# Joining two words of a weight: the low word's top bits made on GpSimd, the join in one VectorE step

## The chip, the cores and the metric

The kernel runs on one core of a Trainium2 chip. The metric is the device time of one execution in microseconds (us); 753.64 us is the median of 3 runs of the kernel before (752.62 to 755.04). TensorE (PE) multiplies, with weight loads (PEld) beside it; VectorE (DVE), ScalarE (ACT) and GpSimd (POOL) do elementwise work; SyncE (SP) issues the DMAs. Every engine takes its own instructions in the order in which they were written and waits on semaphores of the others.

## The reference

Three layers follow one another. Inputs are float32; the weight matrices of both networks reach the chip as float64 (two 32-bit words a number).

```python
scores = scale * np.matmul(q, k.transpose(0, 1, 3, 2))     # 4 batches, 8 heads, 576 x 576, dim 64
attn = softmax(where(local mask or strided mask, scores, -1e9))
x = np.matmul(attn, v)                                      # 2304 x 512 after the heads are joined
h = np.maximum(np.maximum(x @ w1, x @ w2), x @ w3)          # 512 -> 768, three gates
x2 = h @ w_out                                              # 768 -> 512
h = x2 @ w_in                                               # 512 -> 2048
g = np.maximum(h, 0.0) + alpha * np.minimum(h, 0.0)
out = g @ moe2_w_out                                        # 2048 -> 512
```

## The kernel before, in words

**Stages.** The first stage, on PE up to about 320 us, is called the weave here. In it PE works through the attention of all four batches and the gate network of batches 0 to 2 (`gate_products`, L577, and `out1_products`, L599), while every weight of the program is converted once. Then `last_net` does batch 3 (L577, L750, L599), and from about 390 us on the second network runs (L1152, L983); it reads its converted weights back from DRAM. GpSimd works only in the masks at the start and, from 329 us on, in sums and splits of the input of the second network (L211, L828).

**Products.** A float32 number is held as two float32r parts, high and low, and a product is three matmuls (high-high, low-high, high-low).

**Converting a weight.** `from_double` adds the steps for a tile of 128 x 512 weights. `fetch` loads 512 KB into a tile of the `raw` ring (3 tiles). `rebase_words` (L448, ACT) rescales the upper word. `join_words` (L452 and L454, DVE) shifts that upper word left by 3 and then ORs in the lower word shifted right by 29: the tile `word` then holds the float32. There are 56 such tiles in all. Then `split_tasks` makes the high part (L253, ACT) and the low part (L256, DVE). The first 24 tiles stay in SBUF as gate and mix weights; of the others, sums of quarters are formed (L521, L560, DVE), and the parts go through a staging ring `wst` of 3 tiles back to DRAM (`wh`, `wo`, `wp`, `ws`).

**What sets the order.** The weave is written by a planner, `Weave.plan`. Each task has an engine with a cost in ns, a position that says how urgent it is, needs, and rings of buffers (8 PSUM banks, 3 raw tiles and so on). The planner walks through time, always takes the engine whose next task can begin first, and emits the tasks in that order; for some tasks it picks ACT or DVE, whichever would end first. The join had a cost of 1050 ns on DVE. `UNREAD` puts 3 and 9 matmuls whose result nobody reads (L359) ahead of two transposes of the first batch.

**Attention of one unit** (a batch, a pair of heads, a half): scores (L314, PE), mask and maximum (L322, DVE), exponential (L329, ACT), normalise (L351 on ACT or L353 on DVE), transposes (L364, PE), copies out of PSUM into `pt` (L253), values (L389, PE), and the split of the result `x` (L253 ACT, L256 DVE). The first gate product needs `x` of six units of batch 0 and one converted weight.

Of the kernel before, what the change touches and what calls it, by code (L numbers as in the profile page):

```python
# [10 lines left out]
F32 = mybir.dt.float32  # L11
F32R = mybir.dt.float32r
U32 = mybir.dt.uint32
AF = mybir.ActivationFunctionType
ALU = mybir.AluOpType

# [31 lines left out]
class Weave:  # L48
# [16 lines left out]
    def add(self, engines, emit, pos, needs=(), gives=(), makes=(), uses=(), mode=None, slack=0):  # L65
        t = len(self.tasks)
        if engines[0][0] != "PE" and any(key in self.banks for key in uses):
            pos -= self.URGENT
        self.banks.update(key for ring, key in makes if ring == "bank")
        self.tasks.append((engines, emit, pos, needs, makes, mode, slack))  # L70
        for ring, key in makes:
            if ring in self.order:
                self.order[ring].append(key)
        for e in gives:
            self.givers.setdefault(e, []).append(t)
        for key in [key for _, key in makes] + list(uses):
            self.users.setdefault(key, []).append(t)
# [19 lines left out]
    def plan(self, seed=None, near=120, change=100, slack=1.0, delay=350, shift=0.0):  # L97

        rng = random.Random(seed)
        sway = [rng.uniform(-shift, shift) if task[2] > -self.URGENT / 2 else 0.0 for task in self.tasks]  # L100
        delays = {"PE": 300, "ACT": delay, "DVE": delay, "SP": 2300}
        self.made = {ring: [] for ring in self.rings}
        free = dict.fromkeys(delays, 0)
        left = [sum(len(self.givers[e]) for e in task[3]) for task in self.tasks]
        at = [0] * len(self.tasks)
        ready = {t for t, n in enumerate(left) if not n}
        done, mode, order = {}, None, []
        while ready:
            options = {}
            for t in ready:  # L110
                engines, _, pos, _, makes, m, wait = self.tasks[t]
                when = self.place(makes, done)
                if when is None:
                    continue
                when = max(when, at[t] + slack * wait)
                best = None
                for e, cost in engines:
                    start = max(when, free[e])
                    if best is None or start + cost < best[0] + best[2]:
                        best = (start, e, cost)  # L120
                start, e, cost = best
                if m is not None:
                    start += change * (m != mode)
                options.setdefault(e, []).append(
                    (start, pos + sway[t] - (m is not None and m == mode), t, cost))
            pick = None
            for e, c in options.items():
                first = min(o[0] for o in c)
                o = min((o for o in c if o[0] <= first + near), key=lambda o: (o[1], o[0], o[2]))
                if pick is None or o[0] < pick[1][0]:  # L130
                    pick = (e, o)
            e, (start, _, t, cost) = pick
            makes, m = self.tasks[t][4:6]
            ready.remove(t)
            order.append((t, e))
            for ring, key in makes:
                self.made[ring].append(key)
            mode = mode if m is None else m
            free[e] = start + cost
            done[t] = start + cost + delays[e]  # L140
            for u in self.takers.get(t, ()):
                left[u] -= 1
                same = e == "PE" == self.tasks[u][0][0][0]
                at[u] = max(at[u], start + cost if same else done[t])
                if not left[u]:
                    ready.add(u)
        assert len(done) == len(self.tasks)
        return order
# [12 lines left out]
def attention_maxout_prelu_kernel(  # L161
# [13 lines left out]
    nc = tc.nc  # L175
# [74 lines left out]
    add, tl = weave.add, {}  # L250
# [13 lines left out]
    def load(kb):  # L264
        return (("SP", 3 * kb),)
# [30 lines left out]
    def attention_tasks(b, cc, hf, pos, step):  # L296
# [22 lines left out]
        for i, (_, _, _, m) in enumerate(tiles):  # L319
# [7 lines left out]
            def exponential(_, i=i):  # L327
                for j in range(2):
                    nc.scalar.activation(tl[ek][:nq, j, i, :nk], tl[ek][:nq, j, i, :nk], AF.Exp,  # L329
                                         bias=tl["nm", u][:nq, j, i:i + 1], scale=-1.0,  # L330
# [13 lines left out]
        for j in range(2):  # L344
            trk, ptk = ("tr", u, j), ("pt", u, j)

            def normalise(engine, j=j):
                e, rc = tl[ek][:nq, j, :n, :nk], tl["rc", u][:nq, j, :n]
                if engine == "ACT":
                    for i in range(n):  # L350
                        nc.scalar.activation(e[:, i], e[:, i], AF.Copy, scale=rc[:, i:i + 1])  # L351
                else:
# [68 lines left out]
    def from_double(key, src, pos, pace, after=()):  # L421

        rk, ak = ("raw", key), ("word", key)  # L430

        def fetch(_):
            raw = tl[rk] = raw_p.tile([P, DM, 2], U32, tag="raw", name="raw")
            nc.sync.dma_start(raw.rearrange("p n t -> p (n t)"), src.bitcast(U32))

        def rebase(_):
            tl[ak] = words_p.tile([P, DM], U32, tag="word", name="word")
            rebase_words(tl[rk], tl[ak])

        add(load(512), fetch, pos - 3 * pace, gives=[rk], makes=[("raw", rk)])  # L440
        add((("ACT", 570),), rebase, pos, needs=[rk, *after], gives=[("up", key)], makes=[("word", ak)],
            uses=[rk])
        add((("DVE", 1050),), lambda _: join_words(tl[rk], tl[ak]), pos, needs=[("up", key)],
            gives=[ak], uses=[rk, ak])
        return ak

    def rebase_words(raw, a):
        nc.scalar.activation(a.bitcast(F32), raw[:, :, 1].bitcast(F32), AF.Prelu, scale=2.0 ** -112,  # L448
                             alpha=-(2.0 ** 32))

    def join_words(raw, a):
        nc.vector.tensor_scalar(out=a, in0=a, scalar1=3, scalar2=None,  # L452
                                op0=ALU.logical_shift_left)
        nc.vector.scalar_tensor_tensor(out=a, in0=raw[:, :, 0], scalar=29, in1=a,  # L454
                                       op0=ALU.logical_shift_right, op1=ALU.bitwise_or)

    def split_tasks(key, ak, view, n, tile_of, pos, makes=(), given=None):

# [11 lines left out]
    def stay_tasks(key, src, pool, pos, pace):  # L470

        def tile_of():
            t = words[key] = pool.tile([P, 2, DM], F32R, tag="w", name="w")
            return t
        ak = from_double(key, src, pos, pace)
        split_tasks(key, ak, lambda a: a, DM, tile_of, pos)
# [22 lines left out]
    def pair_tasks(s, pos, pace):  # L499

        layer, q = divmod(s, NQ)
        ek, ok = (from_double(("in", layer, f), w2[f, layer], pos + pace * (f - 2 * q), pace,
                              [("sums", s - 2)] if s > 1 else ())
                  for f in (2 * q, 2 * q + 1))
# [4 lines left out]
        def sums(_):  # L509
            for k in sk:  # L510
                tl[k] = words_p.tile([P, DM], U32, tag="word", name="word")
            (e1, e2), (a1, a2), (c1, c2), (d, _) = (
# [28 lines left out]
    def factor_tasks(k, pos):  # L541
# [4 lines left out]
        for key, gk in zip(keys, (("gate", 2 * p, g), ("gate", 2 * p + 1, g))):  # L546
            def recover(_, key=key, gk=gk):
                tl[key] = words_p.tile([P, DM], U32, tag="word", name="word")
                w = words[gk].bitcast(F32)
                nc.vector.tensor_tensor(out=tl[key].bitcast(F32), in0=w[:, 0], in1=w[:, 1], op=ALU.add)  # L550
# [3 lines left out]
        def sums(_):  # L554
            tl[keys[2]] = words_p.tile([P, DM], U32, tag="word", name="word")
            (e1, e2), (a1, a2), (c1, c2) = ((t[:, :half], t[:, half:]) for t in
                                            (tl[key].bitcast(F32) for key in keys))
            for out_, x, y, op in ((c1, e1, a1, ALU.subtract), (a1, a1, a2, ALU.add),
                                   (c2, a1, e1, ALU.subtract), (a2, e2, c2, ALU.subtract)):
                nc.vector.tensor_tensor(out=out_, in0=x, in1=y, op=op)  # L560
# [360 lines left out]
    def temp():  # L921
        return tq.tile([P, HALF], F32, tag="t", name="t")
# [174 lines left out]
    def hidden(n, j, half, h):  # L1097

        f = 2 * (n % NQ) + j
        a = acts[j, half] = temp()  # L1100
        nc.scalar.activation(a, h, AF.Relu, scale=-1.0)  # L1101
        nc.scalar.activation(a, a, AF.Copy, scale=nalpha[:, f:f + 1])  # L1102

# [190 lines left out]
```

## Time and profile before

| | |
|---|---|
| median of 3 runs | 753.64 us (752.62 to 755.04) |
| the profiled execution's own time | 756.32 us |
| its span | 754.50 us, so 1.82 us lie around it |
| granted clock of PE over the span | 0.998 of full |
| PE busy | 737.3 us, 98% |
| VectorE busy | 630.6 us, 84% |
| ScalarE busy | 462.5 us, 61% |
| GpSimd busy | 53.3 us, 7% |
| first matmul | 4.82 us, first gate product 38.72 us |

The span is the time from the first to the last instruction that the profiler saw. Busy shares are means over stages with unlike limits, so the stretches have to be looked at one by one. A row of the timeline reads: start, length, engine, line, operation, output and inputs, shapes, count, and in brackets the idle time before it with what ended it. A row by line reads: count, then busy time in us and mean ns of one, then idle time before the group.

### The profile page before, as it was taken

How to read it: one execution, taken by the hardware profiler on the slowest of the kernel's cores; microseconds unless marked ns; L12 is line 12 of the kernel's file. 1: busy time of each engine (PE TensorE's matmuls, PEld its weight loads, DVE VectorE, ACT ScalarE, POOL GpSimd, SP SyncE). 2: the span in 40 equal slices, each digit the busy share in tenths (PEclk: the TensorE clock that was granted, in tenths of full speed). 3: DMA queues.
4: the chain of work that ended last, by engine and by line, in shares of the span. 5: the costliest groups of instructions: out<-in, count | busy, mean ns of one | idle time of the engine just before them, and what ended most of it. 6: DMA issues, size and time to landing. Idle time of an engine off the chain costs nothing.

```text
span 754.5 us, 16222 instructions
## 1 busy us (share of the span) xinstructions
PE 737.3 (98%) x5680; PEld 718.6 (95%) x5680; DVE 630.6 (84%) x1663; ACT 462.5 (61%) x1249; POOL 53.3 (7%) x64
## 2 busy tenths in 40 slices
PE   5899999999999999999999999999999999999998
PEld 4699999999989999999999999999999999999997
DVE  4899899898988899658869988887988886888885
ACT  5997789567775777423346566634666654556561
POOL 1000000000000000023503010000301000000000
PEclk9999999999999999999999999999999999999999
DMA  7477759996899965778899789999888999877362
GB/s 245 152 242 226 233 197 342 325 326 252 294 338 292 324 243 184 245 291 287 303 324 398 243 297 315 387 387 371 303 288 309 344 400 376 272 240 263 107 198 72
DMA packets 88929, 211.97 MB, mean 281 GB/s; under 512 B 11024, under 2 KB 41232, under 8 KB 88848
## 3 DMA queue, kind: packets, MB, share of 16 engines
q1 hardware_dynamic: 88848, 210.94, 80.2%
q8 instruction: 45, 0.74, 0.4%
q14 instruction: 36, 0.29, 0.1%
HBM read 154.80 MB, written 56.10 MB: 280 GB/s over the span
## 4 chain that ended last, share of the span: by engine, by line
PE 65%; DVE 12%; ACT 10%; DMA 9%; issue 3%; SPq 1%; DVEq 0%; ACTq 0%
PE ph L1152 21%; PE po L983 19%; PE bank L577 10%; PE bank L750 4%; PE bank L599 4%; DMA raw<-in_w 4%; PE ph L983 3%; ACT e L329 3%; DVE word L454 2%; DVE w L256 2%; ACT word L448 1%; PE bank L314 1%; DVE word L452 1%; DVE e L322 1%; DMA wh<-w 1%
## 5 line engine op out<-in xcount | busy, mean ns | idle before, releaser
L1152 PE MATMUL ph<-x,w 128*128 128x384 f32 x990 | 200.4, 338 | 0.2
L577 PE MATMUL bank<-x,w 128*128 128x288 f32 x1440 | 197.2, 296 | 0.0
L577 PEld LDWEIGHTS bank<-x,w 128*128 128x128 f32 x1440 | 191.8, 188 | 1.8
L983 PE MATMUL po<-w,g 128*128 128x256 f32 x1296 | 181.1, 281 | 0.0
L983 PEld LDWEIGHTS po<-w,g 128*128 128x128 f32 x1296 | 174.9, 189 | 0.3
L1152 PEld LDWEIGHTS ph<-x,w 128*128 128x128 f32 x990 | 165.2, 188 | 1.2 <-ACT c L1162 0.4
L1158 DVE TENSOR_TENSOR c<-ph,c 128x384 f32<-128x384 f32 x165 | 89.4, 554 | 35.6 <-PE ph L1152 31.5
L976 ACT CAST g<-c 128x384 fp32r<-128x384 f32 x93 | 47.0, 506 | 90.4 <-DVE c L1136 51.4
L599 PE MATMUL bank<-h,w 128*128 128x288 f32 x576 | 80.8, 300 | 0.5 <-DVE nm L322 0.5
L599 PEld LDWEIGHTS bank<-h,w 128*128 128x128 f32 x576 | 78.2, 191 | 1.4 <-DVE nm L322 0.7
L329 ACT ACTIVATE e<-e,nm 96x128 f32<-96x128 f32 (+2 forms) x176 | 68.5, 403 | 10.0 <-DVE nm L322 10.0
L253 ACT CAST w<-word 128x512 fp32r<-128x512 f32 x100 | 57.6, 591 | 27.3 <-DMA wh<-w 11.8
L256 DVE TENSOR_TENSOR w<-word,w 128x512 fp32r<-128x512 f32 x100 | 63.0, 641 | 10.7 <-ACT w L253 10.3
L1101 ACT ACTIVATE c<-c 128x384 f32<-128x384 f32 x96 | 50.5, 526 | 32.1 <-DVE c L1158 30.7
L1105 DVE SCALAR_TENSOR_TENSOR c<-c 128x384 f32<-128x384 f32 x96 | 56.4, 587 | 8.6 <-ACT c L1102 8.6
L1102 ACT ACTIVATE c<-c,nalpha 128x384 f32<-128x384 f32 x96 | 59.2, 617 | 3.1
L977 DVE TENSOR_TENSOR g<-c,g 128x384 fp32r<-128x384 f32 x96 | 56.2, 585 | 1.9 <-ACT g L976 1.9
L448 ACT ACTIVATE word<-raw 128x512 f32<-128x512 f32 x56 | 37.9, 685 | 22.1 <-DMA raw<-in_w 17.9
L977 DVE TENSOR_TENSOR g<-k,g 128x384 fp32r<-128x384 f32 x72 | 37.2, 557 | 8.0 <-ACT g L976 8.0
L454 DVE SCALAR_TENSOR_TENSOR word<-raw,word 128x512 uint32<-128x512 uint32 x56 | 38.8, 692 | 1.9
L1136 DVE TENSOR_TENSOR k<-c 128x384 f32<-128x384 f32 x72 | 39.9, 582 | 0.0
L976 ACT CAST g<-k 128x384 fp32r<-128x384 f32 x72 | 33.3, 513 | 7.9 <-PE po L983 4.0
(99 smaller groups left out, 834.7 us busy)
## 6 DMA issues: line engine op xcount, KB each, us to landing
w<-wh SPq DMA_DIRECT2D x72, 512.0 KB, 5.4
raw<-in_w SPq DMA_DIRECT2D x50, 512.0 KB, 5.0
w<-wo SPq DMA_DIRECT2D x48, 512.0 KB, 6.1
w<-wp SPq DMA_DIRECT2D x36, 512.0 KB, 6.9
wh<-w SPq DMA_DIRECT2D x24, 512.0 KB, 5.1
xd<-xst SPq DMA_DIRECT2D x28, 384.0 KB, 6.0
x<-xd SPq DMA_DIRECT2D x28, 384.0 KB, 8.1
ws<-w SPq DMA_DIRECT2D x12, 512.0 KB, 4.3
```

Of the source, the lines that this page charges most:

```text
L253: (nc.scalar.copy if e == "ACT" else nc.vector.tensor_copy)(out_, in_)
L256: nc.vector.tensor_tensor(out=out_, in0=x, in1=y, op=ALU.subtract)
L329: nc.scalar.activation(tl[ek][:nq, j, i, :nk], tl[ek][:nq, j, i, :nk], AF.Exp, bias=tl["nm", u][:nq, j, i:i + 1], scale=-1.0, accum_out=tl ...
L577: nc.tensor.matmul(acc, words["gate", f, g][:, wi, cc * P:(cc + 1) * P], xt[b, cc, hf][:, xi, :], start=n == 0, stop=n == 3 * NCC - 1)
L599: nc.tensor.matmul(acc, words["mix", f][:, wi, dc * P:(dc + 1) * P], st["h", hf, f][:, xi, :], start=n == 0, stop=n == 3 * NF1 - 1)
L976: cast(g[:, 0], x)
L977: return g, lambda: nc.vector.tensor_tensor(out=g[:, 1], in0=x, in1=g[:, 0].bitcast(F32), op=ALU.subtract)
L983: nc.tensor.matmul(bank[:, NH * half:NH * (half + 1)], g[:, gi, t * P:(t + 1) * P], w[:, wi, off:off + NH], start=first and i == 0, stop=l ...
L1102: nc.scalar.activation(a, a, AF.Copy, scale=nalpha[:, f:f + 1])
L1105: nc.vector.scalar_tensor_tensor(out=a, in0=h, scalar=0.0, in1=a, op0=ALU.max, op1=ALU.add)
L1152: nc.tensor.matmul(bank, words["h", n, i][:, wi, off + c * P:off + (c + 1) * P], x2h[blk, k, c][:, xi, :], start=m == 0, stop=m == 5)
L1158: nc.vector.tensor_tensor(out=out_, in0=bank, in1=other, op=ALU.add)
```

## The change

GpSimd gets a new step for each of the 56 tiles. `top_bits` reads the top byte of each lower word (8-bit, every eighth byte of the raw tile), multiplies it by 1/32, subtracts 15.5/32 and writes the result as a whole number into the lower word's place; these are the three top bits of that word. The join on DVE is then one instruction: the upper word shifted left by 3, ORed with what GpSimd wrote. The join needs both ScalarE's and GpSimd's step. The planner gets an engine POOL, a cost of 750 for the new step, and 610 in place of 1050 for the join.

```diff
-        delays = {"PE": 300, "ACT": delay, "DVE": delay, "SP": 2300}
+        delays = {"PE": 300, "ACT": delay, "DVE": delay, "POOL": delay, "SP": 2300}
...
-        add((("DVE", 1050),), lambda _: join_words(tl[rk], tl[ak]), pos, needs=[("up", key)],
+        add((("POOL", 750),), lambda _: top_bits(tl[rk]), pos, needs=[rk, *after], gives=[("top", key)], uses=[rk])
+        add((("DVE", 610),), lambda _: join_words(tl[rk], tl[ak]), pos, needs=[("up", key), ("top", key)],
             gives=[ak], uses=[rk, ak])
...
+    def top_bits(raw):
+        top = raw.rearrange("p n t -> p (n t)").bitcast(U8).rearrange("p (n b) -> p n b", b=8)[:, :, 3]
+        nc.gpsimd.tensor_scalar(out=raw[:, :, 0], in0=top, scalar1=2.0 ** -5, scalar2=-15.5 / 32,
+                                op0=ALU.mult, op1=ALU.add)
+
     def join_words(raw, a):
-        nc.vector.tensor_scalar(out=a, in0=a, scalar1=3, scalar2=None,
-                                op0=ALU.logical_shift_left)
-        nc.vector.scalar_tensor_tensor(out=a, in0=raw[:, :, 0], scalar=29, in1=a,
-                                       op0=ALU.logical_shift_right, op1=ALU.bitwise_or)
+        nc.vector.scalar_tensor_tensor(out=a, in0=a, scalar=3, in1=raw[:, :, 0],
+                                       op0=ALU.logical_shift_left, op1=ALU.bitwise_or)
```

Lines behind the change stand 1 to 5 numbers later in the kernel after. Because costs changed, the planner writes the weave in another order on every engine; from `last_net` on the order is the same. Three places follow, before and after apart.

The first is PE in the first batch, from the nine unread matmuls on (k,q: scores; ident,e: transposes; pt,v: values; x,w: gate products). Before:

```order
L359 MATMUL bank<-ident_r 128x512 x9
L364 MATMUL bank<-ident,e 128x96 x6
L314 MATMUL bank<-k,q 108x108 x6
L389 MATMUL bank<-pt,v 64x96 x6
L364 MATMUL bank<-ident,e 128x96 x6
L314 MATMUL bank<-k,q 126x126 x4
L389 MATMUL bank<-pt,v 64x96 x6
L364 MATMUL bank<-ident,e 128x96 x6
L314 MATMUL bank<-k,q 108x108 x6
L389 MATMUL bank<-pt,v 64x96 x6
L577 MATMUL bank<-x,w 128x288 x240
```

And after the change:

```order
L360 MATMUL bank<-ident_r 128x512 x9
L365 MATMUL bank<-ident,e 128x96 x6
L315 MATMUL bank<-k,q 108x108 x6
L365 MATMUL bank<-ident,e 128x96 x6
L390 MATMUL bank<-pt,v 64x96 x6
L315 MATMUL bank<-k,q 126x126 x4
L390 MATMUL bank<-pt,v 64x96 x6
L582 MATMUL bank<-x,w 128x288 x12
L365 MATMUL bank<-ident,e 128x96 x6
L315 MATMUL bank<-k,q 108x108 x6
L390 MATMUL bank<-pt,v 64x96 x6
L582 MATMUL bank<-x,w 128x288 x228
```

One pair of transposes now stands ahead of a pair of values, and the first gate product (12 matmuls) ahead of the last transposes and values of the first batch.

The second is VectorE at the first join of a weight (e,rc: normalise; word: the join). Before:

```order
L353 TENSOR_TENSOR e<-e,rc 96x384 x2
L340 TENSOR_SCALAR rc<-sm 96x6
L341 RECIPROCAL rc<-rc 96x6
L452 TENSOR_SCALAR word<-word 128x512
L454 SCALAR_TENSOR_TENSOR word<-raw,word 128x512
L353 TENSOR_TENSOR e<-e,rc 96x384
```

And after:

```order
L354 TENSOR_TENSOR e<-e,rc 96x384 x2
L341 TENSOR_SCALAR rc<-sm 96x6
L342 RECIPROCAL rc<-rc 96x6
L459 SCALAR_TENSOR_TENSOR word<-word,raw 128x512
L354 TENSOR_TENSOR e<-e,rc 96x384 x2
```

The shift is gone, and a normalise that ScalarE did (three L351 instructions) has come over to VectorE.

The third is PE where the third output layer of the weave begins (h,w: output products, 18 matmuls each). Before:

```order
L314 MATMUL bank<-k,q 108x108 x6
L389 MATMUL bank<-pt,v 64x96 x12
L364 MATMUL bank<-ident,e 128x96 x12
L599 MATMUL bank<-h,w 128x288 x18
L389 MATMUL bank<-pt,v 64x96 x12
L599 MATMUL bank<-h,w 128x288 x54
L577 MATMUL bank<-x,w 128x288 x96
```

And after:

```order
L315 MATMUL bank<-k,q 108x108 x6
L390 MATMUL bank<-pt,v 64x96 x12
L365 MATMUL bank<-ident,e 128x96 x12
L315 MATMUL bank<-k,q 126x126 x4
L582 MATMUL bank<-x,w 128x288 x12
L390 MATMUL bank<-pt,v 64x96 x12
L604 MATMUL bank<-h,w 128x288 x54
L582 MATMUL bank<-x,w 128x288 x24
```

Scores and a gate product stand where the first output product stood.

## Rows read from the trace of the kernel before

**Rows 1.** Busy time by stretch: length, then PE, PEld, DVE, ACT, POOL, clock, DMA

```profile
20.00:40.00 20.00, 17.18 (x185) 13.35 (x186) 18.06 (x103) 20.00 (x88) 0.00 (x0) 1.00 0.52 172
40.00:300.00 260.00, 258.14 (x2167) 248.09 (x2167) 237.60 (x744) 194.51 (x616) 0.00 (x0) 0.99 0.81 274
200.00:220.00 20.00, 18.50 (x165) 17.46 (x165) 18.44 (x54) 13.47 (x46) 0.00 (x0) 0.91 0.99 342
329.00:590.00 261.00, 260.69 (x1829) 259.46 (x1828) 215.25 (x430) 137.89 (x289) 49.77 (x47) 1.00 0.90 322
```

**Rows 2.** Waits of PE up to 330 us: us in total, times, longest

```profile
PE bank L314 <- DMA k<-in_kTs: 5.9, 2, 4.8
...
PE bank L364 <- ACT e L351: 0.4, 1, 0.4
```

**Rows 3.** Timeline of PE at the end of the first batch's attention

```profile
36.69 0.47 PE L364 MATMUL bank<-ident,e 96*128 96x96 f32 x3 [0.56 <-DVE e L353]
...
38.72 32.10 PE L577 MATMUL bank<-x,w 128*128 128x288 f32 x240
```

**Rows 4.** Timeline of PE at the third output layer

```profile
214.17 0.47 PE L364 MATMUL bank<-ident,e 96*128 96x96 f32 x3 [1.02 <-DVE t L667]
215.12 4.13 PE L599 MATMUL bank<-h,w 128*128 128x288 f32 x18 [0.48 <-DVE nm L322]
```

**Rows 5.** Timeline of ACT and DVE just before that

```profile
212.40 0.62 ACT L253 CAST w<-word 128x512 fp32r<-128x512 f32 x1 [2.49 <-DMA wo<-w]
...
213.06 0.69 DVE L256 TENSOR_TENSOR w<-word,w 128x512 fp32r<-128x512 f32 x1 [1.03 <-ACT w L253]
```

**Rows 6.** DVE by line and shape, 40 to 300 us

```profile
L256 DVE TENSOR_TENSOR w<-word,w 128x512 fp32r<-128x512 f32 x78 | 52.5, 683 | 3.9 <-ACT w L253 3.6
L454 DVE SCALAR_TENSOR_TENSOR word<-raw,word 128x512 uint32<-128x512 uint32 x52 | 36.0, 692 | 1.8
L521 DVE TENSOR_TENSOR word<-word 128x256 f32<-128x256 f32 x60 | 24.7, 422 | 1.3
L452 DVE TENSOR_SCALAR word<-word 128x512 uint32<-128x512 uint32 x52 | 21.8, 420 | 4.2 <-ACT word L448 4.1
L256 DVE TENSOR_TENSOR h<-t,h 128x288 fp32r<-128x288 f32 x35 | 15.8, 452 | 2.1 <-ACT h L673 2.1
L560 DVE TENSOR_TENSOR word<-word 128x256 f32<-128x256 f32 x24 | 10.2, 423 | 0.6
```

**Rows 7.** Timeline of DVE: two joins one after the other

```profile
41.14 0.42 DVE L452 TENSOR_SCALAR word<-word 128x512 uint32<-128x512 uint32 x1
41.59 0.69 DVE L454 SCALAR_TENSOR_TENSOR word<-raw,word 128x512 uint32<-128x512 uint32 x1
```

**Rows 8.** POOL by line and shape

```profile
L211 POOL TENSOR_TENSOR xst<-xs,xst 128x384 fp32r<-128x384 f32 x16 | 17.6, 1099 | 43.6 <-ACT xst L208 43.5
L976 POOL CAST g<-c 128x384 fp32r<-128x384 f32 x3 | 1.7, 572 | 31.2 <-PE ph L1152 29.4 <-DVE c L1105 1.8
L190 POOL CAST ident_r<-ident 128x128 fp32r<-128x128 f32 x1 | 0.3, 291 | 0.1
```

**Rows 9.** DVE by line, 329 to 590 us, where GpSimd works

```profile
L1105 DVE SCALAR_TENSOR_TENSOR c<-c 128x384 f32<-128x384 f32 x59 | 35.9, 609 | 5.0 <-ACT c L1102 4.9
L977 DVE TENSOR_TENSOR g<-c,g 128x384 fp32r<-128x384 f32 x58 | 35.2, 607 | 0.6 <-ACT g L976 0.6
L730 DVE TENSOR_TENSOR t<-t 128x288 f32<-128x288 f32 x16 | 9.7, 604 | 0.4
```

**Rows 10.** DVE by line, 600 to 700 us, where GpSimd rests

```profile
L1105 DVE SCALAR_TENSOR_TENSOR c<-c 128x384 f32<-128x384 f32 x27 | 14.9, 553 | 2.3 <-ACT c L1102 2.3
L977 DVE TENSOR_TENSOR g<-c,g 128x384 fp32r<-128x384 f32 x26 | 14.3, 552 | 0.6 <-ACT g L976 0.6
```

**Rows 11.** Timeline of ACT, 31.5 to 39.5 us

```profile
33.42 0.66 ACT L253 CAST w<-word 128x512 fp32r<-128x512 f32 x1
...
34.80 0.75 ACT L448 ACTIVATE word<-raw 128x512 f32<-128x512 f32 x1
```

More of the change, by code (lines that the diff above doesn't have):

```diff
@@ L13 @@
 U32 = mybir.dt.uint32
+U8 = mybir.dt.uint8
 AF = mybir.ActivationFunctionType
```

## The prediction

> **What bounds the kernel now.** Start with the page's busy times by engine, then the busy times by stretch. From 40 to 300 us, where all weights but the first are converted, PE is busy 258.14 of 260 us and VectorE 237.60 [rows 1]. So VectorE is nearly full but PE is what time hangs on: a microsecond of VectorE's counts only where PE waits for it. The waits of PE come next. The largest, 5.9 us, is for the first loads [rows 2], which the change does not touch. In the run up to the first gate product at 38.72 us [rows 3] ScalarE is busy 20.00 of 20 us, VectorE 18.06 and PE 17.18 [rows 1]: a chain through all three, ScalarE the fullest. Then PE runs 240 gate matmuls in 32.10 us [rows 3], 134 ns each.
>
> Behind 40 us little is left to win. PE waits 0.4 us for a normalise [rows 2], 1.02 us for transposes and 0.48 us for an output product at 214 us [rows 4]. After that pair of waits the granted clock of the stretch is 0.91 [rows 1], and 18 matmuls take 4.13 us [rows 4] where 18 x 134 ns = 2.41 us would do: part of the stretch ran at 1.2 and not 2.4 GHz, which cost 1.72 us. In all 0.4 + 1.02 + 0.48 + 1.72 = 3.6 us. What stood behind the waits at 214 us is not VectorE's load: VectorE idled 1.03 us for a cast of ScalarE's, and ScalarE had idled 2.49 us for the landing of a store to `wo` [rows 5], since the staging ring's tile was not free.
>
> **The change part by part: VectorE's load.** Each join loses its shift. Its start lies 0.45 us ahead of the OR [rows 7], so between 40 and 300 us 52 x 0.45 = 23.4 us go [rows 6]. The OR stays: same shape, two inputs in SBUF, 692 ns [rows 6].
>
> What comes back is told by the stage where GpSimd works today. With GpSimd at rest L1105 takes 553 ns and L977 552 [rows 10]; from 329 to 590 us, with GpSimd busy 49.77 us [rows 1], they take 609 and 607 [rows 9]. L730 with both inputs in SBUF takes 604 [rows 9], against 452 of the same shape in L256 [rows 6]. So GpSimd's work costs VectorE 59 x 56 + 58 x 55 + 16 x 152 ns = 8.9 us, 0.18 us for each us of GpSimd's. These three groups are 35.9 + 35.2 + 9.7 - 8.9 = 71.9 us, 0.275 of their 261 us. In the weave five of the six groups shown have two SBUF inputs (all but L452): 52.5 + 36.0 + 24.7 + 15.8 + 10.2 = 139.2 us, 0.535 of 260. Scaled by 0.535 / 0.275, an us of GpSimd's costs VectorE an estimated 0.35 us there.
>
> The Trainium skill (SBUF — State Buffer, section "Who interferes with whom") speaks against the change here: a VectorE instruction with two SBUF inputs and a GpSimd instruction that reads SBUF exclude each other, and the later one waits for the other's whole length. By that rule a VectorE instruction that meets a new GpSimd step waits for all that is left of it. The rows above agree in direction; they give the mean price.
>
> How long the new step takes no row shows. The nearest is a cast with one input: 572 ns for 384 elements, 291 for 128 [rows 8], 1.10 ns an element, so an estimated 0.71 us for 512. Below, the 384-element cast itself, 0.57. Above, the two-input 1099 ns [rows 8] by 512/384: 1.47 us. I take 0.71, as the step has one input. The Trainium skill (GPSIMD Engine Reference, section "Performance versus the Vector engine") measured 769 ns for a tight loop over 512 elements; by it the load below would be 14.0 and not 12.9 us.
>
> So 52 x 0.71 x 0.35 = 12.9 us return (10.4 to 26.8): VectorE's load falls by 10.5 us (13.0 less to 3.4 more) of 237.6. Half of what the diff seems to take away is given back. The step turns into a burden from 0.45 / 0.35 = 1.29 us on.
>
> GpSimd has nothing else to do before 329 us. Its step starts when the raw tile has landed, as L448 does on ScalarE, but not behind ScalarE's queue, so the join should find it done; where both start together it takes 0.71 against ScalarE's 0.75 us [rows 11]: nothing. Behind a join that did wait stand VectorE's PSUM readers, which free banks for PE; the bound for that is in the rivals. SP's queue keeps its loads; a raw tile comes free 0.45 us earlier, and a fetch waits for it, a gain that DMA, 0.81 busy [rows 1], may keep: 0.
>
> **The start.** The order has PE do the first gate product ahead of the last transposes and values. I followed the order by hand from 30 us on, with each instruction as long as in the timeline of before. The last input of that product, an x split on VectorE, comes near 35.85 us; PE waits about 0.65 us for it and multiplies until 37.45, the transposes and scores follow until 38.95. The last values then wait for copies that ScalarE makes behind a rebase (0.75) and a weight's cast (0.66) [rows 11], until about 39.65, and the other gates go on at 40.55 with 12 x 0.134 = 1.6 us done: as if they had begun at 38.95. Against 38.72 [rows 3] that is +0.2 us. Ends: -1.5 if ScalarE's lost normalise lets it run earlier than I follow, +2 if a wait in that chain is missed.
>
> **The later waits.** Of the 3.6 us the stretch at 214 us has 3.2. Its releaser is a store, and stores are as many and as large as before; but the order there is new (a gate product and scores where the first output product stood), so the same meeting of store, cast and bank need not recur. Ends: -3.6 (none recurs) and +3.2 (one more like it). The rows point at DMA, so I take -0.8.
>
> Sum: +0.2 - 0.8 = -0.6 us on the span of 754.50. The profiled execution took 756.32 with 1.82 us around the span, 2.7 above the median; the difference is applied to the median: 753.64 - 0.6 = 753.0.
>
> **Rivals.**
> A. As summed: VectorE's relief is mostly off the path, 753.0, its own range 751.4 to 755.9, no change.
> B. The relief reaches PE: the start gains 1.3 us (ScalarE is the fullest there and gives a normalise away) and the waits of 3.6 us go: 753.64 - 4.9 = 748.7; half of it 751.2. For it speaks that PE's late waits end with VectorE instructions [rows 4], against it what stood behind them [rows 5].
> C. The port: the step takes over 1.29 us, VectorE's load rises, and in stretches as full as 200 to 220 us (18.44 of 20 [rows 1]) its PSUM readers L667 and L322 come late, banks run out, and PE waits 1.02 + 0.48 and loses 1.72 of clock each time, 3.2 us. One or two such places: 756.8 to 760.0. Slower. For it speaks the two-input row, against it the cast's.
> D. The new order by itself: the load is right, but one place of the reordered attention starves PE as 214 us did: 753.64 + 3.2 = 756.8. Nothing in the rows excludes it, and a gate product ahead of waiting values (start) is of that kind.
> That the step does nothing for VectorE (back to the old load at 1.29 us) gives the order's effect alone and lies in A.
>
> **How the numbers follow.** A 0.47, B 0.29, C 0.12, D 0.12. About 2.3 us (0.3%) is what a measurement can tell from no change; A lies inside, B beyond it below, C and D above: faster 0.29, same 0.47, slower 0.24. The range 749.0 to 757.5 takes in most of B, A, D and the low end of C; about 2 in 10 lie outside.
>
> **What would show it.** Right: the new step near 0.7 us, longer where it meets VectorE; L256 and L521 with means some 5 to 15% up while PSUM readers keep theirs; VectorE busy about 227 us between 40 and 300; first gate product near 36 us, and the second one near 40.5; PE as busy as before. Wrong: a step above 1.3 us; PE waits for L667 or L322 at several places; or PE without waits behind 40 us and a start that is a microsecond or more shorter.

## The result and the profile after

The change makes the kernel slower: 758.7 us (median of 6, 757.36 to 760.22) against 753.13 (6 runs, 751.39 to 755.04), a ratio of 1.0066 with a 95% interval of 1.0049 to 1.0084. (Ratios are those on record; they are not the quotients of the medians, which here would be 1.0074.) That is the direction of the rivals C and D, inside C's 756.8 to 760.0 and above D's 756.8, and beyond the range of 749.0 to 757.5. The profiled execution took 760.22 us with a span of 758.4, 3.9 more than the span of before. The medians are 5.6 us apart, since before's profiled execution lay 3.2 us above its median and after's 1.5.

Busy time by stretch in the kernel after; the columns are length, PE, PEld, DVE, ACT, POOL, clock, DMA share and GB/s:

```profile
20.00:40.00 20.00, 17.19 (x178) 13.10 (x176) 18.12 (x97) 20.00 (x87) 0.65 (x1) 1.00 0.54 180
40.00:300.00 260.00, 253.68 (x2146) 243.54 (x2147) 234.51 (x710) 195.53 (x618) 44.84 (x52) 1.00 0.82 283
200.00:220.00 20.00, 18.36 (x165) 17.49 (x164) 16.23 (x57) 11.63 (x38) 2.49 (x3) 1.00 0.81 281
329.00:590.00 261.00, 260.02 (x1830) 259.06 (x1829) 213.16 (x428) 136.63 (x288) 49.95 (x47) 1.00 0.89 323
```

Read it against [rows 1]. Between 40 and 300 us PE is busy 4.5 us less, though VectorE, which the change was to relieve, is 3.1 us less busy too. Nothing got fuller; PE waits more. The waits of PE in that stretch, in total us, times and longest:

```profile
PE bank L365 <- DVE t L672: 1.9, 2, 1.3
PE bank L365 <- ACT e L352: 1.1, 1, 1.1
PE bank L315 <- DVE nm L323: 1.1, 1, 1.1
PE bank L390 <- ACT pt L254: 1.1, 1, 1.1
PE bank L582 <- ACT t L669: 1.0, 1, 1.0
PE bank L582 <- DVE t L672: 0.6, 1, 0.6
PE bank L604 <- DVE nm L323: 0.5, 1, 0.5
```

Before, PE waited 1.9 us there, at two places. Now the rows make 7.3 us, at six places (0.9 us of the first wait lie ahead of 40 us). The timeline of PE shows the start and four of the others:

```profile
35.70 1.86 PE L582 MATMUL bank<-x,w 128*128 128x288 f32 x12
...
40.13 1.00 PE L390 MATMUL bank<-pt,v 128*64 128x96 f32 x12 [1.06 <-ACT pt L254]
41.07 8.20 PE L582 MATMUL bank<-x,w 128*128 128x288 f32 x60
...
84.94 1.32 PE L582 MATMUL bank<-x,w 128*128 128x288 f32 x8 [0.97 <-ACT t L669]
...
122.43 0.47 PE L365 MATMUL bank<-ident,e 96*128 96x96 f32 x3 [1.33 <-DVE t L672]
123.37 2.65 PE L604 MATMUL bank<-h,w 128*128 128x288 f32 x18 [0.48 <-DVE nm L323]
...
218.74 0.82 PE L315 MATMUL bank<-k,q 64*126 64x126 f32 x8 [1.08 <-DVE nm L323]
...
286.38 0.81 PE L365 MATMUL bank<-ident,e 96*128 96x96 f32 x6 [1.14 <-ACT e L352]
```

The first product began at 35.70 us, but the gates went on at 41.07 with 12 matmuls done, as if they had begun at 39.47: 0.75 us later than in [rows 3]. The last values of the first batch waited 1.06 us for ScalarE's copies, as followed from the order. The waits behind that make 6.2 us against the 3.6 us of before, in which 1.72 us were the clock's. A wait of 0.72 us at 540 us, outside the weave, does the rest: 0.75 + (6.2 - 3.6) + 0.72 = 4.1 us, against the 3.9 by which the span grew. This accounts for the two profiled executions and not for the whole 5.6 us between the medians.

The change's own instructions, by line and shape; first GpSimd's new step over the whole span (count, then busy time in us and mean ns of one, then idle time before it and what ended it):

```profile
L455 POOL TENSOR_SCALAR raw<-raw 128x512 uint32<-128x512 uint8 x56 | 47.5, 848 | 224.4 <-DMA raw<-in_w 121.1 <-ACT e L330 31.2 <-DVE word L526 23.1
```

And VectorE's from 40 to 300 us, to be held against [rows 6]:

```profile
L257 DVE TENSOR_TENSOR w<-word,w 128x512 fp32r<-128x512 f32 x82 | 57.7, 710 | 5.3 <-ACT w L254 5.0
L459 DVE SCALAR_TENSOR_TENSOR word<-word,raw 128x512 uint32<-128x512 uint32 x52 | 37.2, 721 | 7.3 <-POOL raw L455 6.5 <-ACT word L450 0.5 <-issue 0.3
L672 DVE TENSOR_TENSOR t<-bank,t 128x288 f32<-128x288 f32 x70 | 31.2, 446 | 2.3 <-ACT e L352 1.0 <-ACT e L330 0.9 <-PE bank L582 0.3
L526 DVE TENSOR_TENSOR word<-word 128x256 f32<-128x256 f32 x64 | 27.9, 446 | 1.5
```

The step takes 707 ns in the median, 848 in the mean. Two-input instructions of VectorE grow by 4 to 6% (683 to 710, 692 to 721, 422 to 446), while L672, which reads PSUM, keeps its 446 to 450. So rival C, a step above 1.29 us and a fuller VectorE, is out by the profile. The sign set for it did come, though: PE waits for L672 and L323 (before the change L667 and L322) at several places, 4.1 of the 7.3 us. What the trace alone can't say is whether the six waits come from the new order or from joins that wait for GpSimd (6.5 us in 11 waits).

### The profile page after: what moved, and what is told of

Same layout as the page of the kernel before. It is cut to its first block, busy times and chain, and to the rows that moved or that the text cites. A ratio compares the mean times of both kernels' runs of the same rounds, so it can differ in the third digit from the quotient of the medians.

```text
span 758.4 us, 16321 instructions
## 1 busy us (share of the span) xinstructions
PE 736.3 (97%) x5680; PEld 717.5 (95%) x5680; DVE 620.6 (82%) x1611; ACT 460.3 (61%) x1241; POOL 100.9 (13%) x120
## 4 chain that ended last, share of the span: by engine, by line
PE 75%; DVE 12%; ACT 5%; DMA 4%; issue 2%; SPq 0%; DVEq 0%; POOL 0%; ACTq 0%; POOLq 0%
PE ph L1157 20%; PE po L988 18%; PE bank L582 17%; PE bank L604 6%; PE bank L755 4%; PE ph L988 3%; PE bank L390 2%; PE bank L315 2%; ACT e L330 2%; DMA raw<-in_w 2%; PE bank L365 2%; DVE e L323 1%; DVE w L257 1%; DVE word L526 1%; DVE g L982 1%
## 5 line engine op out<-in xcount | busy, mean ns | idle before, releaser
L604 PE MATMUL bank<-h,w 128*128 128x288 f32 x576 | 79.1, 296 | 0.5 <-DVE nm L323 0.5
L455 POOL TENSOR_SCALAR raw<-raw 128x512 uint32<-128x512 uint8 x56 | 47.5, 848 | 224.4 <-DMA raw<-in_w 121.1
L257 DVE TENSOR_TENSOR w<-word,w 128x512 fp32r<-128x512 f32 x100 | 65.6, 663 | 5.8 <-ACT w L254 5.5
L459 DVE SCALAR_TENSOR_TENSOR word<-word,raw 128x512 uint32<-128x512 uint32 x56 | 39.7, 718 | 7.3 <-POOL raw L455 6.5
```

The costliest lines, as they stand in the source:

```text
L257: nc.vector.tensor_tensor(out=out_, in0=x, in1=y, op=ALU.subtract)
L604: nc.tensor.matmul(acc, words["mix", f][:, wi, dc * P:(dc + 1) * P], st["h", hf, f][:, xi, :], start=n == 0, stop=n == 3 * NF1 - 1)
```

## The experiments

Each was timed in turn with the kernel before on one chip; before's median lay between 752.87 and 753.74 us. Lines of an experiment's kernel may stand a few numbers off.

**Order and instructions apart.** Theory 1: the new order costs the time. Theory 2: GpSimd's step does. Four kernels tell them apart. In the first the order of after is kept and the old instructions are put in:

```diff
-        add((("POOL", 750),), lambda _: top_bits(tl[rk]), pos, needs=[rk, *after], gives=[("top", key)], uses=[rk])
+        add((("POOL", 750),), lambda _: None, pos, needs=[rk, *after], gives=[("top", key)], uses=[rk])
...
     (join_words: shift, then shift and OR, as before)
```

> Order of the kernel after, instructions of the kernel before (no step on GpSimd, the join is shift and OR again). Theory 1, the new order costs the 5 us: about 758 us, 756 to 761, with PE waits near 40, 85, 122, 218, 279 and 286 us again; VectorE's extra 23 us of shifts may add to it. Theory 2, the step on GpSimd costs them (its time in the join's way, and the shared interface): 753, 751.5 to 754.5.

Measured: 761.97 us, ratio 1.0125 (1.0097 to 1.0152). Theory 1. With no step on GpSimd at all the order is even worse, with VectorE's shifts back (busy 242.12 us from 40 to 300 us). PE's waits for VectorE's L323 and L674 there make 3.1 us: rival C's sign comes without rival C's cause. In the second the order of before is kept on PE, ScalarE and SyncE, with the new instructions:

```diff
             rebase_words(tl[rk], tl[ak])
+            top_bits(tl[rk])
...
     (join_words: one step, as after; the planner's prices as before)
```

> Order of the kernel before on PE, ScalarE and SyncE, instructions of the kernel after (the step on GpSimd is written behind the rebase, the join is one step). Theory 1, order: 753 or a little less, 751 to 754, since VectorE is relieved by about 10 us. Theory 2, the step on GpSimd: 757 to 760.

Measured: 752.85 us, ratio 0.9991 (0.9975 to 1.0008): no loss. Theory 2 falls for this order. Its profile, busy time by stretch:

```profile
40.00:300.00 260.00, 258.67 (x2202) 248.77 (x2202) 231.15 (x694) 199.22 (x626) 42.97 (x52) 1.00 0.81 277
```

VectorE's wait for GpSimd's step (total us, times, longest):

```profile
DVE word L459 <- POOL raw L455: 6.6, 9, 1.6
```

And its lines of VectorE from 40 to 300 us, with GpSimd's:

```profile
L257 DVE TENSOR_TENSOR w<-word,w 128x512 fp32r<-128x512 f32 x79 | 55.7, 715 | 7.3 <-ACT w L254 7.1
L526 DVE TENSOR_TENSOR word<-word 128x256 f32<-128x256 f32 x60 | 26.9, 458 | 1.3
L455 POOL TENSOR_SCALAR raw<-raw 128x512 uint32<-128x512 uint8 x56 | 45.7, 816 | 233.2 <-DMA raw<-in_w 130.1 <-DVE rc L342 20.2 <-DVE w L257 20.0
```

The joins wait for GpSimd as long as in the kernel after (6.6 us), the neighbours grow as much (715, 458), and PE is busy 258.67 us, as before the change. At 213 us PE waits at the place of [rows 4] again:

```profile
213.05 0.47 PE L365 MATMUL bank<-ident,e 96*128 96x96 f32 x3 [0.85 <-DVE t L672]
214.00 2.68 PE L604 MATMUL bank<-h,w 128*128 128x288 f32 x18 [0.48 <-DVE nm L323]
```

But the 18 products behind the waits take 2.68 us and not 4.13, so the loss of clock in before's profile need not come with this order.

In the third, the kernel after leaves out GpSimd's step, so that its weights are other numbers:

```diff
-        add((("POOL", 750),), lambda _: top_bits(tl[rk]), pos, needs=[rk, *after], gives=[("top", key)], uses=[rk])
+        add((("POOL", 750),), lambda _: None, pos, needs=[rk, *after], gives=[("top", key)], uses=[rk])
...
-                                       op0=ALU.logical_shift_left, op1=ALU.bitwise_or)
+                                       op0=ALU.logical_shift_left, op1=ALU.bitwise_and)
```

> Order and join of the kernel after, with GpSimd's step left out (the low words stay as loaded and the join ANDs them in, so the weights' numbers are others; the instructions that are left are as many and as long). Theory 1, order: 757 to 759, waits at the same places. Theory 2, the step on GpSimd: 752 to 754. If both have a part, this lies between, and 758.7 minus this is GpSimd's part.

Measured: 756.12 us, ratio 1.0028 (1.0009 to 1.0047), with single runs from 751.56 to 758.04. It lies between: in after's order the step costs 758.7 - 756.1 = 2.6 us, and 2.4 us of loss are left without it. Its kept trace is that of the fastest run (751.56), so it can't show where the others lose. The fourth changes nothing but the planner's number in the kernel before:

```diff
-        add((("DVE", 1050),), lambda _: join_words(tl[rk], tl[ak]), pos, needs=[("up", key)],
+        add((("DVE", 1055),), lambda _: join_words(tl[rk], tl[ak]), pos, needs=[("up", key)],
```

> The kernel before with the planner's cost of the join at 1055 in place of 1050; the instructions are the same, the order of the weave is another in some 25 rows of PE. Theory 1, the order alone moves the time by microseconds, whatever the reason for a new order: it differs from before, anywhere from 750 to 759. Theory 2 has no reason for a difference: 753, 752 to 754.5.

Measured: 755.48 us, ratio 1.0034 (1.0015 to 1.0053). Five nanoseconds in a plan moved the kernel by 0.34%. In its profile the weave is better than before (busy time by stretch):

```profile
40.00:300.00 260.00, 259.63 (x2210) 250.09 (x2209) 241.69 (x754) 198.52 (x627) 0.00 (x0) 1.00 0.81 277
```

The loss stands at the border to the second network, where ScalarE's copy into `xo` came late, having itself waited 1.96 us for the transfer `x<-xo` (timelines of ScalarE and of PE):

```profile
391.67 0.40 ACT L806 COPY xo<-bank 128x288 f32<-128x288 f32 x1 [1.96 <-DMA x<-xo]
392.12 1.14 PE L1152 MATMUL ph<-x,w 128*128 128x384 f32 x5 [3.41 <-ACT xo L806]
```

**Is it the start, the price, or chance?** In the next the first gate product waits for the first batch's last values, so that PE's start is that of before:

```diff
-                needs=xks + [("gate", f, g)] + ([("begun", g - 1, tk)] if g else []),
+                needs=xks + [("gate", f, g)] + ([("begun", g - 1, tk)] if g else [])
+                + ([("x", 0, 1, 1)] if n == b == 0 else []),
```

> The kernel after, where the first gate product also needs the last x of the first half-batch, so that PE has the transposes, scores and values of the first batch ahead of all gate products, as before the change; the rest is planned anew. Theory 1, the order's waits add up place by place: the wait of 1.06 us near 40 us goes, 0.7 us or so are won, 757 to 758.5, the later waits stay. Rival, the start sets off all the later waits: 753 to 755.

Measured: 759.68 us, ratio 1.0092 (1.0079 to 1.0105). Both expectations missed: the wait at 40 us went, but one of 1.37 us came at 35 us, and most of the later ones stayed. The gates began at 37.70 us, a microsecond earlier than before the change, and the kernel was no faster for it. The start alone is not what makes the order bad; the edit also moved instructions behind the start.

The next two change only the planner's price of the join in the kernel after (610 to 860, 610 to 605), and one more that of before (1050 to 1040). The first as a diff, the others alike:

```diff
-        add((("DVE", 610),), lambda _: join_words(tl[rk], tl[ak]), pos, needs=[("up", key), ("top", key)],
+        add((("DVE", 860),), lambda _: join_words(tl[rk], tl[ak]), pos, needs=[("up", key), ("top", key)],
```

> The kernel after with the planner's cost of the join at 860 in place of 610, which adds what GpSimd's steps cost VectorE elsewhere. Theory 1a, the planner's prices were too low for VectorE and so it packed the order too tightly: 753 to 755. Theory 1b, any new order is a draw of a few us, and a price that fits better helps little: 755 to 760, with waits at 218 and 280 us again.

Measured: 755.12 us, ratio 1.0035 (1.0016 to 1.0054).

> The kernel after with the planner's cost of the join at 605 in place of 610: a neutral second draw. Theory 1a (prices): as after, 757.5 to 760. Theory 1b (draws): anywhere from 753 to 762, by more than an interval from after.

Measured: 755.68 us, ratio 1.0047 (1.0028 to 1.0065).

> The kernel before with the planner's cost of the join at 1040 in place of 1050: another neutral draw of the old instructions. Theory 1b (draws): 751 to 758; theory 1a (prices): 752.5 to 755, since the price is as true as before.

Measured: 754.2 us, ratio 1.0020 (1.0008 to 1.0031). A redraw by 5 ns (605) moved after by 3 us, as much as the step to 860 did: price and chance can't be told apart by these.

**The instructions' part in other orders.** The new instructions were put into the orders of 1055 and 1040 as in the second experiment, and the old ones into that of 605 as in the first.

```diff
     (1055 and 1040)
             rebase_words(tl[rk], tl[ak])
+            top_bits(tl[rk])
...
     (605)
-        add((("POOL", 750),), lambda _: top_bits(tl[rk]), pos, needs=[rk, *after], gives=[("top", key)], uses=[rk])
+        add((("POOL", 750),), lambda _: None, pos, needs=[rk, *after], gives=[("top", key)], uses=[rk])
```

> The order of the run with the join priced 1055, the new instructions (GpSimd's step behind the rebase, join in one step). If the instructions' own part is a gain in any order: 752 to 754.8, that is 0.7 to 3.3 us under the 755.5 of that order with the old instructions. If GpSimd's step is neutral or hurts: 755 to 758.

> The order of the kernel after with the join priced 605, the old instructions. If the instructions' own part is a gain in any order and more in a tight one: 757 to 760 against 755.7 with the new ones. If it is not: 754.5 to 756.5.

> The order of the run with the join priced 1040, the new instructions. Gain in any order: 751 to 753.6, against 754.2 with the old ones, and perhaps below both kernels. No gain: 754 to 756.

Measured: 753.14 (ratio 0.9994, 0.9975 to 1.0013), 761.71 (1.0103, 1.0077 to 1.0128) and 754.09 us (1.0007, 0.9992 to 1.0021). In the order of 1040 the gain that was expected is not there. All pairs together, medians in us:

| order planned with | old instructions | new instructions |
|---|---|---|
| 1050, before's | 753.1 to 753.7 | 752.85 |
| 1055 | 755.48 | 753.14 |
| 1040 | 754.20 | 754.09 |
| 610 and GpSimd's task, after's | 761.97 | 758.7 |
| 605 and GpSimd's task | 761.71 | 755.68 |

Down a column one reads the order, along a row the instructions. In every row the new ones are no slower by the medians: they win 2.3 to 6.0 us where the old instructions are well above 753, and next to nothing in the orders of 1050 and 1040. The order of after costs 5.9 us with the new instructions and some 8.5 with the old.

**Does the order wait for stores?** ScalarE stood 5.0 us behind a store at 212 us in the kernel after (timeline of ScalarE):

```profile
212.23 0.62 ACT L254 CAST w<-word 128x512 fp32r<-128x512 f32 x1 [5.00 <-DMA ws<-w]
```

So the planner was told that a DMA takes longer:

```diff
-        delays = {"PE": 300, "ACT": delay, "DVE": delay, "POOL": delay, "SP": 2300}
+        delays = {"PE": 300, "ACT": delay, "DVE": delay, "POOL": delay, "SP": 4600}
```

> The kernel after with the planner's time from a DMA's issue to its landing at 4600 in place of 2300 (the trace has 4 to 7 us). If the new order is worse since its casts stand ahead of stores that have not landed (ScalarE idled 5.0 us for one at 212 us): 753 to 756, with ScalarE's waits for wh, wo, wp and ws halved. If orders are draws whose quality has nothing to do with this price: anywhere from 754 to 761, those waits as long as before.

Measured: 763.83 us, ratio 1.0129 (1.0107 to 1.0151), the slowest of all and above both expectations. Busy time in its stretch from 40 to 300 us:

```profile
40.00:300.00 260.00, 259.60 (x2231) 250.16 (x2230) 224.56 (x695) 191.71 (x616) 38.05 (x49) 1.00 0.77 261
```

And PE's timeline behind the stretch:

```profile
335.05 2.29 PE L582 MATMUL bank<-x,w 128*128 128x288 f32 x8 [5.02 <-DVE t L593]
```

Half of it came as expected: ScalarE's waits for stores fell from 22.9 us (9.4, 7.9, 2.9 and 2.7 for `ws`, `wh`, `wp` and `wo`) to 5.2 (none, 1.9, 2.7 and 0.6), and PE waited 0.4 us in the weave. But only 49 of the 52 steps of GpSimd are done there; conversions moved to the weave's end, and PE paid 5.02 us in one wait.

**Price against task.** Three kernels more change the price of the join with GpSimd's task planned as in after (1050, 1060, 1300); one has the step hidden behind the rebase, as in the second experiment, with the price 610. The last as a diff from the kernel after:

```diff
             rebase_words(tl[rk], tl[ak])
+            top_bits(tl[rk])
...
-        add((("POOL", 750),), lambda _: top_bits(tl[rk]), pos, needs=[rk, *after], gives=[("top", key)], uses=[rk])
-        add((("DVE", 610),), lambda _: join_words(tl[rk], tl[ak]), pos, needs=[("up", key), ("top", key)],
+        add((("DVE", 610),), lambda _: join_words(tl[rk], tl[ak]), pos, needs=[("up", key)],
```

> The kernel after with the join priced 1050 as before the change; GpSimd's step is planned as in the change. If the price of 610 made the order bad: 752 to 754.5, with under 2 us of PE waits between 40 and 300 us. If the task on GpSimd in the plan did: 756 to 760. If chance: anything in 752 to 760.

> New instructions, GpSimd's step not planned as a task but written behind the rebase, the join priced 610. If the price made the order bad: 756 to 760. If the task on GpSimd in the plan did: 752 to 754.5.

> As the run with the join priced 1050, now 1060: a neutral redraw with some 58 rows of PE elsewhere. Price: 752 to 755 again. Chance: 752 to 760, by more than an interval from the run at 1050.

> The kernel after with the join priced 1300, well over what it and its step cost VectorE. If a higher price only loosens the order: 751.5 to 754, perhaps the best of all. If a price that is off in either direction hurts: 754 to 758.

Measured: 753.63 (ratio 1.0002, 0.9984 to 1.0020), 757.54 (1.0052, 1.0032 to 1.0071), 757.41 (1.0040, 1.0024 to 1.0055) and 754.51 us (1.0011, 1.0000 to 1.0022). The stretch from 40 to 300 us of the four, in this order, one fence each:

```profile
40.00:300.00 260.00, 259.74 (x2211) 250.02 (x2211) 231.73 (x695) 200.57 (x631) 43.01 (x52) 1.00 0.81 277
```

```profile
40.00:300.00 260.00, 255.12 (x2147) 244.87 (x2146) 234.02 (x710) 195.41 (x617) 40.89 (x52) 0.99 0.83 283
```

```profile
40.00:300.00 260.00, 256.82 (x2155) 246.83 (x2154) 232.60 (x700) 198.27 (x625) 42.48 (x52) 0.99 0.82 279
```

```profile
40.00:300.00 260.00, 260.00 (x2207) 249.66 (x2206) 224.06 (x681) 201.80 (x643) 42.05 (x52) 1.00 0.79 271
```

The task on GpSimd with the price 1050 is harmless; the price 610 without the task costs PE nearly as much as after's 6.3 us (4.9). So it is not the task. But the two kernels are hardly new draws of the order. Counted in the traces, the first has some 90 of 1248 of ScalarE's instructions elsewhere than before, and the second some 130 of 1240 elsewhere than after; the redraws by 5 ns (1055 and 605) moved some 300 and 640. PE's waits in the kernel with the price 610 and no task are in the main those of after again:

```profile
PE bank L582 <- DVE t L672: 1.2, 1, 1.2
PE bank L315 <- DVE nm L323: 1.1, 1, 1.1
PE bank L390 <- ACT pt L254: 1.1, 1, 1.1
PE bank L365 <- ACT e L352: 1.0, 1, 1.0
PE bank L365 <- DVE t L672: 0.8, 2, 0.6
PE bank L315 <- DMA k<-in_kTl: 0.8, 1, 0.8
```

Whether a low price makes any order bad, or this one order is bad, the crossing therefore can't tell. VectorE's load speaks for the price: at 1050 VectorE is busy 231.7 us and PE idles 0.3, at 610 VectorE 234.0 and PE 4.9, at 1300 VectorE 224.1 and PE nothing. Two runs speak against it as the whole cause. With the old instructions and 1055 VectorE was busy 241.69 us, and PE idled 0.4. At 1060, a neutral redraw, PE idles 3.2 us, most of it at the place of [rows 4], with the slow products behind it (clock of 200 to 220 us 0.94):

```profile
216.14 0.47 PE L365 MATMUL bank<-ident,e 96*128 96x96 f32 x3 [1.91 <-DVE t L672]
217.09 4.18 PE L604 MATMUL bank<-h,w 128*128 128x288 f32 x18 [0.48 <-DVE nm L323]
```

With the new instructions the prices 605 and 610 gave 755.7 to 758.7 us, 860 gave 755.1, and those from 1040 to 1300 gave 752.9 to 754.5, but for the 757.4 of 1060: a tendency, and not shown to be more. None of the versions beats the kernel before by more than its interval.

## Why the prediction was wrong, point by point

**PE bounds, VectorE's load is mostly off the path: right in the old order alone.** There a load that fell by 6.5 us (237.60 to 231.15) brought 0.9 us by the medians, and 1.9 at most by the interval. In three of the five orders of the table the new instructions won 2.3 to 6.0 us.

**VectorE's net relief, 10.5 us: too large.** With the order unchanged it was 6.5, with the change as written 3.1, since VectorE got more normalises (40 to 42 in the whole weave) and copies (5 to 7) from ScalarE. Of the 23.4 us that were to go, only the shifts' own 21.8 [rows 6] were busy time; the rest was the gap between shift and OR. What GpSimd's steps give back is the growth of VectorE's other instructions. Added up by line and shape from before to the second experiment, it is some 9.6 us (L257 at 128x512 2.5 of it, 79 x 32 ns), 0.22 us for each of the 42.97 us of the step and not 0.35. So the price of the later stage, 0.18, came nearer without the scaling. Of the 16.9 us between 23.4 and 6.5 that leaves some 6 whose cause stays open; a part is two instructions more in the stretch than the lost shifts explain (694 against 744 - 52).

**The step, 0.71 us: right** (median 707 ns; the mean, 848, holds steps of up to 2.82 us). **The join finds it done: wrong**, 6.5 us of waits for GpSimd where nothing was predicted; the waits for ScalarE's rebase in turn fell from 4.1 [rows 6] to 0.5. In the old order 6.6 us of such waits cost nothing that can be measured, in the new one the step's whole presence cost 2.6 us. VectorE's two-input lines grew by 4 to 6%, at and under the lower edge of the 5 to 15% that were given as a sign.

**The start, +0.2 us: right in mechanism, too small.** Product at 35.70 (predicted 35.85), values at 40.13 (39.65), gates at 41.07 (40.55), so +0.75. The gap: ScalarE's chain ran half a microsecond later than I followed it. The wait of 0.65 us ahead of the product did not come; PE got there later.

**The later waits, -0.8 us: the step that failed.** I treated the new order as a fresh draw centred on the old one's waits, with an end of +3.2, one more place like 214 us. The waits grew from 3.6 to 6.2 us at five places, and another 0.7 us fell behind the weave: +3.3 us in place of -0.8. The 3.6 us were no firm base either: 1.72 of them were the clock's, a loss that the second experiment did not have in the same order. Rival D, with a part of 0.12, is what came, and dearer than its one place. A warning stood in the diff: the price 610 told the planner that a join is 440 ns shorter, while VectorE's load per join fell by 6.5 us / 52 = 125 ns in the old order. I had worked out that half of the relief comes back and never put that number against the planner's price. The run with the price 610 and no task, 757.54, against 752.85 at 1050 shows that the order planned with this price loses without the task. How much of it is the price and how much chance stays open: 605 and 1060 each lie 3 to 4 us from their neighbours.

**The clock:** the 1.72 us of before did not recur in the profiled execution of after, and the granted clock of 200 to 220 us was 1.00. A pair of waits did recur: 1.33 and 0.48 us at 122 and 123 us, with 0.47 us of transposes between them as at 214 us before, and the 18 products behind took 2.65 us. Of the four such pairs shown, this one and that of the second experiment (0.85 and 0.48, then 2.68) came without a loss, and that of before (1.02 and 0.48, then 4.13) and that at the price 1060 (1.91 and 0.48, then 4.18) with one. What tells them apart is not shown.

## What to carry to other kernels

When a change alters the prices of a planner, first put the new price against what the instruction really costs the engine, with what it takes from its neighbours; a price that is too low may pack the order until the bound engine waits, which these runs suggest and don't show. Then separate order and instructions: run the new instructions in the old order. And where the plan is greedy, a redraw by a neutral amount tells how far a result is the order's luck: here 0.2 to 0.5%, against an effect of 0.7%. A redraw is one only if the order did change: compare the two orders, and not the prices.

## What the runs showed of the hardware that I had not expected

GpSimd can be the one that is held. At 58 us of the kernel after a step took 1.99 us, while VectorE's join and weight split beside it took 0.68 us each, as long as before the change (timelines of GpSimd and of VectorE):

```profile
58.39 1.99 POOL L455 TENSOR_SCALAR raw<-raw 128x512 uint32<-128x512 uint8 x1 [0.44 <-DVE e L354]
```

```profile
58.59 0.68 DVE L459 SCALAR_TENSOR_TENSOR word<-word,raw 128x512 uint32<-128x512 uint32 x1
59.19 0.68 DVE L257 TENSOR_TENSOR w<-word,w 128x512 fp32r<-128x512 f32 x1
```

Both sides pay: in the second experiment VectorE's other instructions grew by the 9.6 us above, and GpSimd's step took 816 ns in the mean against the 0.65 us of its first run at 14 us.

The 8-bit input, read from every eighth byte, and the conversion to whole numbers show no cost of their own: 0.65 us in the steps of the first 17 us, less than the 0.71 estimated from casts of 32-bit numbers.
